# Decode step in one kernel: the last loads of K and V merged and put in the order K7, V6, V7

## The chip, the cores and the metric

The kernel runs on 1 core of one Trainium2 chip. The metric is device time in microseconds, the median of repeated runs. One further execution was recorded by the hardware profiler; all rows below come from it.

## The reference

One token of 512 elements passes through an attention block with a cache and a small feed-forward block, both under a modulation computed from `c`. Everything is bf16.

```python
mod = (_silu(c) @ w_mod).reshape(c.shape[0], 6, 1, -1)        # sa, ca, ga, sb, cb, gb
h = _layernorm(x) * (1 + ca) + sa
q = h @ wq                                                    # 32 query heads of 128
k, v = the caches of 8 heads, 32768 positions each, repeated 4 times
p = softmax(q k^T * 128 ** -0.5);  o = p v
x = x + ga * (o @ wo)                                         # wo: 4096 x 512
h = _layernorm(x) * (1 + cb) + sb
x = x + gb * (relu(h @ w1) @ w2)                              # w1: 512 x 1792, w2: 1792 x 512
```

K and V of one cache head are 8 MB each, so the 8 heads are 128 MB; w_mod, wq, wo, w1 and w2 together are some 15 MB.

## The kernel before, in words

**The stream of loads.** All large loads are issued by SyncE (SP) from one list, `stream` (L162 to L169), one after the other, through `load` (L112) and `stream_dma` (L154; the issue itself is L155). They go into a ring of three buffers of 8 MB (`piece`, L106): w_mod and wq share the first, then come K and V of the heads, and the last buffer, `tail_sb`, takes wo, w1 and w2. A load is issued when the buffer's former content has been used up. Which buffer that is follows from the order: K7 follows V4, V6 follows K6, V7 follows V5, and `tail_sb` follows K7. A head's K or V has four quarters (`u` = 0 to 3). Heads 0 to 4 are loaded whole, K5 too; K6, V5, K7 and V6 are loaded in halves, V7 in a half and two quarters. K7 and V6 alternate: K7's first half, V6's first half, K7's second, V6's second. wo comes in four transfers (4, 2, 1 and 1 heads, `WOP`, L47), w1 in one, w2 in five (`W2P`, L52).

**K0's second half** is loaded in three pieces (`UNEVEN`, L57 and L137 to L142): all but the last 512 bytes of each row, then these bytes of 111 rows, then those of the other 17. The vectors c and x come in one transfer each, issued by ScalarE (ACT, L183).

**One head.** VectorE (DVE) turns K in place (`turn_k`, L441), a quarter at a time, of K7 an eighth at a time. TensorE (PE) forms the scores with 16 matmuls for a quarter (`scores`, L460). `softmax` (L468) takes the maximum (L473; for K7 a maximum of each bank, L466, and then L475), sends it over the partitions (L478, L492), takes the exponential on ACT (L497), turns the result on DVE (L502) and sums it (L506, L509). Then PE multiplies with V, 16 matmuls for a quarter (`pv`, L523). `blocks` (L552, L556) scales the outcome on DVE, `o_cols` (L560) puts it in columns, and once all heads of a part of wo are done, `normalise` (L574) and `spread` (L586, L590) prepare it for that part.

**The order of work.** PE and DVE follow the order of the program from L637 on, written out by hand. In the loop over heads 0 to 5, head g+1's scores come before head g's `pv`. Then head 7 and 6 follow by hand (L675 to L708): K7's first two quarters are turned and scored, PE does `pv` of V6's first two quarters (L691), K7's other quarters follow, then head 7's softmax with the rest of V6 around it, and then V7.

**The end.** `project(i)` multiplies part i of wo: the first two parts into rows (L599), the other two into columns (L605), and `join_rows` (L614; L617, L622) turns the rows and adds them to the columns. Behind that come the residual (L740, L741, tile x1T), the second layer norm, w1 (L765), the relu (L775, L776), w2 (L788) and the output (L793, L795, L796). `keep_clock(n)` (L630, L635) puts n spare matmuls between these steps, whose results are not used.

Of the kernel before, what the change touches and what calls it, by code (L numbers as in the profile page):

```python
# [17 lines left out]
def kernel(  # L18
# [14 lines left out]
    nc = tc.nc  # L33
    P = 128
    _, _, D = A_x.shape
    _, Hkv, Sk, Dh = A_k_cache.shape
# [6 lines left out]
    TK = 64  # L43
    NTILE = Sk // (P * TK)
    NG = NTILE // 2

    WOP = [(0, Hkv // 2), (Hkv // 2, Hkv // 4), (Hkv - 2, 1), (Hkv - 1, 1)]  # L47
    WOROWS = 2
    LAST = Hkv - 1
    LOOPED = Hkv - 2  # L50
    HALVED = LOOPED - 1
    W2P = [(0, 5), (5, 10), (10, 12), (12, 13), (13, 14)]  # L52
    W1P = [(0, KT)]

    OUT0, OUT1 = 30, 34

    UNEVEN, EDGE, MOST = ("k", 0, (2, 3)), 2 * TK * Dh - D // 2, 111  # L57
    SPACE = 14
    assert Dh == 128 and REP == 4 and D == 512 and FT == W2P[-1][1] and NTILE == 4
    scale = float(Dh) ** -0.5  # L60
# [101 lines left out]
    whole, halves = [(0, 1, 2, 3)], [(0, 1), (2, 3)]  # L162
    stream = [("k", 0, halves[0]), ("wm",), ("wq",), ("k", 0, halves[1])]
    for g in range(LOOPED):
        stream += [("k", g + 1, s) for s in (halves if g >= HALVED else whole)] + [("v", g, s) for s in (halves if g >= HALVED else whole)]
    for s in halves:
        stream += [("k", LAST, s), ("v", LOOPED, s)]
    stream += [("v", LAST, (0, 1)), ("v", LAST, (2,)), ("v", LAST, (3,))] + [("wo", i) for i in range(len(WOP))]
    stream += [("w1", i) for i in range(len(W1P))] + [("w2", i) for i in range(len(W2P))]  # L169
    pos = [0]  # L170

# [8 lines left out]
    wm_sb = need(("wm",))  # L180
    cx_row = const.tile([16, D // 8], BF16)
    for i, row in enumerate((c[0], A_x[0, 0])):
        nc.scalar.dma_start(out=cx_row[8 * i:8 * i + 8], in_=row.rearrange("(a n) -> a n", a=8))  # L183

    ident_bf = const.tile([P, P], BF16)
    make_identity(nc, ident_bf[:])
# [10 lines left out]
        out=sel.rearrange("p (h par) (a c) -> p h par a c", h=2, a=4),  # L197
        in_=AP(ib.tensor, ib.offset, [ib.ap[0], [64, 2], [1, 2], [0, 4], [2, 32]]),
# [8 lines left out]
        out=mask16.rearrange("p (s q) -> p s q", q=REP),  # L207
        in_=AP(ident_f[:].tensor, ident_f[:].offset, [ident_f[:].ap[0], [0, 4], [1, REP], [REP, P // REP]]),
# [4 lines left out]
    for n in sorted({n * REP for _, n in WOP}):  # L213
        cmask[n] = const.tile([P, P // n], F32, name=f"cmask{n}")
        nc.vector.tensor_reduce(
            out=cmask[n][:], in_=ident_f[:].rearrange("p (c r) -> p c r", r=n), op=ALU.add, axis=AX.X,
# [3 lines left out]
            out=rsel_f[:], in_=ident_f[:].rearrange("p (c r) -> p r c", r=n), op=ALU.add, axis=AX.X,  # L220
# [6 lines left out]
        out=smask[:], in_=ident_f[0:16, 0:16].rearrange("p (s q) -> p s q", q=REP), op=ALU.add, axis=AX.X,  # L227
# [7 lines left out]
        out=place32[:], in_=ident_f[:].rearrange("p (j m) -> p m j", m=32), op=ALU.add, axis=AX.X,  # L235
# [4 lines left out]
        out=rowpick[:, OUT0:OUT1], in_=ident_f[:].rearrange("p (j m) -> p j m", m=32), op=ALU.add, axis=AX.X,  # L240
# [8 lines left out]
        out=cx_bd, in0=cx_row[:].unsqueeze(1).to_broadcast([16, 8, D // 8]),  # L249
# [23 lines left out]
    def row_bank(t):  # L273

        nc.vector.memset(t, 0.0)
        return t
# [85 lines left out]
    def four_rows(e, name):  # L362
# [16 lines left out]
        out=nca[:], in0=modT_sb[:, KT:2 * KT], scalar1=-1.0, scalar2=-1.0, op0=ALU.mult, op1=ALU.add,  # L379
# [3 lines left out]
        out=ncb[:], in0=modT_sb[:, 4 * KT:5 * KT], scalar1=-1.0, scalar2=-1.0, op0=ALU.mult, op1=ALU.add,  # L383
# [18 lines left out]
    for i in range(2):  # L402
        nc.vector.transpose(out=q_cols[:, i, :], in_=q_ps[i])
        nc.scalar.copy(
            out=qT_sb[:, 16 * i:16 * (i + 1)], in_=q_cols[:, i, :].rearrange("p (h r) -> p h r", r=32)[:, :, 0],
# [109 lines left out]
    def pv(g, us, js=range(16)):  # L515

        nb = 4 if g == HALVED - 1 else 1

        PT_g = PT_tiles[g][:].rearrange("p (h j c) -> p h (j c)", h=2, c=32)
        Vs = [need(("v", g, u)) for u in us]  # L520

        def step(u, V, PT, Vx, first=False):
            nc.tensor.matmul(o_tiles[g][:], lhsT=PT, rhs=Vx, start=first, stop=False, skip_group_check=True)  # L523

        Vf = [V.rearrange("p (s j) d -> p s (j d)", s=4) for V in Vs]
        if looped(g, us):

            with tc.tile_critical() as section:
                last_loop[:] = loop[:] = [section.name]
                with nc.tensor.Fori(0, 512 - 32 * nb + 1, 32 * nb) as at:  # L530
                    for b in range(nb):
                        for u, V in zip(us, Vf):
                            step(u, V, PT_g[:, u // 2, 32 * b + 16 * (u % 2):][:, bass.DynSlice(at, 16)],
                                 V[:, :, Dh * b:][:, :, bass.DynSlice(at * (Dh // 32), Dh)])
        else:
            for u, V in zip(us, Vf):
                for j in js:
                    c0 = 32 * j + 16 * (u % 2)
                    step(u, V, PT_g[:, u // 2, c0:c0 + 16], V[:, :, Dh * j:Dh * (j + 1)], (u, j) == (0, 0))
# [8 lines left out]
    def blocks(g):  # L548

        o = o_tiles.pop(g)[:].rearrange("p (s d) -> p s d", s=4)  # L550
        Y = spool.tile([16, Dh], F32, tag="Y", name="Y", bufs=1)
        nc.vector.scalar_tensor_tensor(  # L552
            out=o, in0=o, scalar=Linv_tiles.pop(g)[:], in1=smask[:].unsqueeze(2).to_broadcast([16, 4, Dh]),
            op0=ALU.mult, op1=ALU.mult,
        )
        nc.vector.tensor_reduce(out=Y[:], in_=o.rearrange("p s d -> p d s"), op=ALU.add, axis=AX.X)  # L556
        Y_tiles[g] = Y
# [24 lines left out]
    def spread(i):  # L582

        n = WOP[i][1] * REP
        o2_ps = small_ps([P, n], "o2_ps")
        nc.tensor.matmul(  # L586
            o2_ps[:], lhsT=oA[i][:].rearrange("p h c -> p (h c)"), rhs=rsel[n][:], start=True, stop=True,
        )
        o2 = const.tile([P, n], BF16, name=f"o2_sb{i}")
        nc.vector.tensor_copy(out=o2[:], in_=o2_ps[:])  # L590
        o2_tiles[i] = o2

    def project(i):

        n = WOP[i][1] * REP
        wo_sb = need(("wo", i))
        for r in range(n):
            if i < WOROWS:
                nc.tensor.matmul(  # L599
                    a_rows[0][32 * (r % 4):32 * (r % 4) + 1, :], lhsT=o2_tiles[i][:, r:r + 1],  # L600
                    rhs=wo_sb[:, r, :], start=False, stop=(i == WOROWS - 1 and r >= n - 4), skip_group_check=True,
                )
                continue
            for ko in range(KT):
                nc.tensor.matmul(  # L605
                    attnT_ps[:, ko:ko + 1],
                    lhsT=wo_sb[:, r, :].rearrange("p (m ko) -> p ko m", ko=KT)[:, ko, :],
                    rhs=o2_tiles[i][:, r:r + 1], start=False, stop=(i == len(WOP) - 1 and r == n - 1),
                    skip_group_check=True,
                )  # L610
# [3 lines left out]
    def join_rows():  # L614

        aT = room("tail_sb", TAIL, [P, 512])
        nc.vector.transpose(  # L617
            out=aT.rearrange("p (a ko m) -> p a ko m", a=4, ko=KT),
            in_=a_rows[0].rearrange("p (a m ko) -> p a ko m", a=4, ko=KT),
        )  # L620
        for a in range(4):
            nc.tensor.matmul(  # L622
                attnT_ps[32 * a:32 * a + 32, :], lhsT=place32[:],
                rhs=aT.rearrange("p (a ko m) -> p a ko m", a=4, ko=KT)[:, a, :, 0],
                start=False, stop=False, skip_group_check=True,
            )
# [3 lines left out]
    def keep_clock(n):  # L630

        if not spare:
            spare.append(bank("spare_ps"))
        for _ in range(n):
            nc.tensor.matmul(spare[0], lhsT=ident_bf[:], rhs=qbd[0][:, :, 0:P], start=True, stop=True)  # L635

    with tc.manual_schedule(engines={mybir.EngineType.PE, mybir.EngineType.DVE}):  # L637
# [37 lines left out]
        g, h = LOOPED, LAST  # L675
# [12 lines left out]
        normalise(g - 1)  # L688
        spread(part_of(g - 1))
        bank_max(h, 0)  # L690
        pv(g, (0, 1))  # L691
        for u in (2, 3):
            for half in range(2):
                turn_k(h, u, half)
# [3 lines left out]
        next(soft)  # L698
        next(soft)
        next(soft)  # L700
        pv(g, (2,), range(6))
        next(soft)
        next(soft)
        open_o(LAST)
        pv(g, (2,), range(6, 16))
        pv(g, (3,))
        next(soft)
        next(soft, None)  # L708
        end_b.append(two_banks("end_ps"))
        a_rows.append(row_bank(end_b[0][:, 0, :]))  # L710
        blocks(g)
        pv(LAST, (0, 1))
        o_cols(LAST - 1)
        normalise(LAST - 1)
        pv(LAST, (2,))
        spread(2)
        hid_ps = ps_o.tile([P, 512], F32, tag="o", name="hid_ps")
        nc.vector.memset(hid_ps[:], 0.0)
        pv(LAST, (3,))
# [6 lines left out]
        keep_clock(2)  # L726
        project(1)
        normalise(LAST)
        spread(3)
        keep_clock(2)  # L730
        project(2)
        keep_clock(1)
        join_rows()
        keep_clock(1)
        project(3)


        stat2 = const.tile([P, 2], F32)
# [3 lines left out]
            out=x1T[:], in0=x1T[:], scalar=1.0, in1=xT, op0=ALU.mult, op1=ALU.add, accum_out=stat2[:, 0:1],  # L742
# [31 lines left out]
        for f0, f1 in ((0, FT // 2), (FT // 2, FT)):  # L774
            nc.vector.transpose(out=hidT[:, f0:f1], in_=hid_v[:, f0:f1])  # L775
            nc.scalar.activation(  # L776
                out=AP(hb.tensor, hb.offset + 32 * f0 + 31, [hb.ap[0], [32, f1 - f0]]),
                in_=hidT[:, f0:f1, 0], func=ACT.Relu,
            )

        for part, (f0, f1) in enumerate(W2P):
            w2_sb = need(("w2", part))
            for ft in range(f0, f1):
                for i in (0, 2, 1, 3):
                    row = OUT0 + i
# [41 lines left out]
```

## Time and profile before

| | us |
|---|---|
| median of 3 runs | 354.11 (354.06 to 354.18) |
| the profiled execution, its own time | 354.42 |
| its span, first to last instruction | 352.6 |
| PE busy / DVE busy / ACT busy | 272.3 / 195.6 / 18.7 |
| mean rate of the loads | 424 GB/s, 149.42 MB read |

The span starts at 0 in all rows. Rows of the timeline give start, duration, engine, line, operation, output and inputs and, in brackets, how long the engine was idle before and what released it. "x32" is the count of merged instructions; the duration of such a row runs from the first to the end of the last.

### The profile page before, as it was taken

To read this page: it belongs to the slowest core of one execution; us is meant where nothing else is said; L and a number is where in the kernel's file an instruction comes from. 1 tells how busy PE (TensorE), PEld (TensorE's weight loads), DVE (VectorE), ACT (ScalarE), POOL (GpSimd) and SP (SyncE) were. 2 spreads that over 40 slices of the span, in tenths; PEclk is the share of its full clock that TensorE was granted. 3 is DMA by queue.
4 is the path that set the end of the run, shared out by engine and by line. 5 is a ranking of instruction groups with operands and counts; after the bars stand their busy time and mean duration, and the time that the engine had idled before them with its cause. 6 is when DMAs were issued, how large, how long until landed. Compare 5 with 4: busy or idle time off the path is not lost. (4 is left out here: it accounts for less than half of the span.)

```text
span 352.6 us, 3544 instructions
## 1 busy us (share of the span) xinstructions
PE 272.3 (77%) x1310; PEld 111.8 (32%) x1310; DVE 195.6 (55%) x167; ACT 18.7 (5%) x37; POOL 6.0 (2%) x26
## 2 busy tenths in 40 slices
PE   0054980695999679884988499976999999789994
PEld 0021330232333224331333233322444443234442
DVE  7662563983079513965099316956674293743142
ACT  1200003001000010001000100001000100011000
POOL 3000000000000000000000000000000000000000
PEclk9996895698999969998999979996999999999999
DMA  8999989999999999999999999999999999999995
GB/s 353 404 432 456 468 387 461 446 401 446 439 424 440 416 439 446 401 455 446 409 453 446 409 453 431 426 394 439 446 414 427 450 429 424 431 453 398 432 426 213
DMA packets 5222, 149.57 MB, mean 424 GB/s; under 512 B 604, under 2 KB 988, under 8 KB 1628
## 3 DMA queue, kind: packets, MB, share of 16 engines
q1 hardware_dynamic: 5180, 149.43, 98.5%
q8 instruction: 8, 0.13, 0.1%
q14 instruction: 2, 0.02, 0.0%
q10 hardware_dynamic: 32, 0.00, 0.0%
HBM read 149.42 MB, written 0.00 MB: 424 GB/s over the span
## 5 line engine op out<-in xcount | busy, mean ns | idle before, releaser
L441 DVE STREAM_TRANSPOSE Ksb<-Ksb 128x4096 f32<-128x4096 f32 (+1 forms) x34 | 131.5, 3912 | 57.6 <-DMA Ksb<-in_A_k_cache_dram 57.6
L460 PE MATMUL S_ps<-Ksb,qbd 128*128 128x512 bf16 x512 | 118.9, 385 | 19.2 <-DVE Ksb L441 18.3
L523 PE MATMUL o_ps<-Vsb,P_g 128*16 (+1 forms) x512 | 124.3, 401 | 10.9 <-ACT P_g L497 10.0
L460 PEld LDWEIGHTS <-qbd 128*128 128x128 bf16 x512 | 49.2, 97 | 84.9 <-issue 27.6
L523 PEld LDWEIGHTS o_ps<-Vsb,P_g 128*16 x320 | 30.4, 95 | 60.0 <-issue 31.8
L523 PEld LDWEIGHTS <-P_g 128*16 128x16 bf16 x192 | 16.7, 90 | 22.9 <-issue 0.4
L473 DVE TENSOR_REDUCE m_p<-S_ps 128x1 f32<-128x1024 f32 x7 | 8.6, 1223 | 21.8 <-PE S_ps L460 21.8
L502 DVE STREAM_TRANSPOSE P_g<-P_g 128x1024 bf16<-128x1024 bf16 x8 | 10.0, 1245 | 15.6 <-ACT P_g L497 15.6
L494 ACT ACTIVATE nbias<-Mb_ps 128x1 f32<-128x1 f32 x8 | 1.4, 171 | 269.5 <-PE Mb_ps L492 269.5
L324 PE MATMUL mod_ps<-wmq_sb,siluT 128*1 128x512 bf16 x24 | 3.6, 624 | 9.9 <-DMA wmq_sb<-in_w_mod_dram 9.9
L332 DVE STREAM_TRANSPOSE Ksb<-Ksb 128x4096 f32<-128x4096 f32 x2 | 8.8, 4424 | 1.7 <-DMA Ksb<-in_A_k_cache_dram 1.7
L478 PE MATMUL mT_ps<-ident_f,m_p 128*1 128x128 f32 x8 | 2.2, 270 | 8.9 <-DVE m_p L473 7.9
L497 ACT ACTIVATE P_g<-S_ps,nbias 128x1024 bf16<-128x1024 f32 x8 | 8.9, 1114 | 0.2
L560 PE MATMUL acc_ps<-mask_sb,Y 16*128 16x4 f32 x16 | 3.4, 282 | 5.1 <-DVE Y L556 5.1
L552 DVE SCALAR_TENSOR_TENSOR o_ps<-o_ps,Linv,smask 16x512 f32<-16x512 f32 x8 | 5.8, 720 | 2.8 <-PE o_ps L523 2.8
L254 PE MATMUL xc_ps<-cx_sel,wmq_sb 16*128 16x2 bf16 x4 | 0.3, 172 | 8.7 <-DVE wmq_sb L248 8.7
L590 DVE CAST o_sb<-o_ps 128x4 bf16<-128x4 f32 (+2 forms) x4 | 0.7, 167 | 11.1 <-PE o_ps L586 11.1
L415 POOL TENSOR_TENSOR qbd<-qrep_sb,rowpick 128x64 bf16<-128x64 bf16 x8 | 2.4, 299 | 228.0 <-PE S_ps L460 198.3
L509 DVE RECIPROCAL Linv<-L_ps 16x1 f32<-16x1 f32 x8 | 1.0, 126 | 8.3 <-PE L_ps L506 8.3
L556 DVE TENSOR_REDUCE Y<-o_ps 16x128 f32<-16x512 f32 x8 | 5.4, 679 | 0.3
L635 PE MATMUL spare_ps<-qbd,ident_bf 128*128 128x512 bf16 x18 | 5.4, 381 | 0.0
L396 PE MATMUL q_ps<-wmq_sb,hT 128*1 128x512 bf16 x32 | 3.6, 626 | 2.3 <-DMA wmq_sb<-in_A_wq_dram 2.3
(114 smaller groups left out, 71.6 us busy)
## 6 DMA issues: line engine op xcount, KB each, us to landing
Ksb<-in_A_k_cache_dram SPq DMA_DIRECT2D x5, 4096.0 KB, 22.9
Vsb<-in_A_v_cache_dram SPq DMA_DIRECT2D x5, 4096.0 KB, 36.5
wmq_sb<-in_A_wq_dram SPq DMA_DIRECT2D x1, 4096.0 KB, 28.1
Vsb<-in_A_v_cache_dram SPq DMA_DIRECT2D x2, 2048.0 KB, 41.1
Ksb<-in_A_k_cache_dram SPq DMA_DIRECT2D x1, 4032.0 KB, 37.2
wmq_sb<-in_w_mod_dram SPq DMA_DIRECT2D x1, 3072.0 KB, 18.9
tail_sb<-in_A_wo_dram SPq DMA_DIRECT2D x1, 2048.0 KB, 23.2
tail_sb<-in_B_w_dram SPq DMA_DIRECT2D x1, 1792.0 KB, 30.6
```

What stands on the lines that cost most here:

```text
L324: nc.tensor.matmul(dst[j // 4][32 * (j % 4):32 * (j % 4) + 1, :], lhsT=src_T[:, kt:kt + 1], rhs=w[:, kt, j * 512:(j + 1) * 512], start=(kt ...
L332: nc.vector.transpose(out=t, in_=t)
L396: nc.tensor.matmul(q_ps[i][32 * a:32 * a + 1, :].rearrange("o (h e) -> o h e", e=32), lhsT=hT[:, kt:kt + 1], rhs=wq_f[:, kt, i, a], start= ...
L441: t = nc.vector.transpose(out=KTt.bitcast(F32), in_=KTt.bitcast(F32))
L460: nc.tensor.matmul(S_ps_tiles[g], lhsT=qbd[g % 2][:, hp, 4 * (7 - s):4 * (7 - s) + P], rhs=KTv[:, 16 * sl:16 * sl + 16, h, :, par], start= ...
L473: behind_loop(nc.vector.reduce_max(out=m_p[:], in_=S_g.rearrange("p g f -> p (g f)"), axis=AX.X))
L497: nc.scalar.activation(out=P_g[:], in_=S_g.rearrange("p g f -> p (g f)"), func=ACT.Exp, bias=nbias[:], scale=scale, accum_out=l_g[:],)
L502: behind_loop(nc.vector.transpose(out=P_g[:], in_=P_g[:]))
L523: nc.tensor.matmul(o_tiles[g][:], lhsT=PT, rhs=Vx, start=first, stop=False, skip_group_check=True)
L552: nc.vector.scalar_tensor_tensor(out=o, in0=o, scalar=Linv_tiles.pop(g)[:], in1=smask[:].unsqueeze(2).to_broadcast([16, 4, Dh]), op0=ALU.m ...
L556: nc.vector.tensor_reduce(out=Y[:], in_=o.rearrange("p s d -> p d s"), op=ALU.add, axis=AX.X)
L635: nc.tensor.matmul(spare[0], lhsT=ident_bf[:], rhs=qbd[0][:, :, 0:P], start=True, stop=True)
```

## The change

Loads: K of head 6 and V of head 5 become one transfer each. The end of the list is K7, V6, V7 in halves, without alternating, and V7's second half is one transfer. wo comes in three transfers (4, 2 and 2 heads), w2 in four. K0's last bytes are split into 123 and 5 rows. c comes in three transfers and x in four. The number of transfers in all stays 40.

Compute: `pv` of V6's first half is taken out of its place between K7's quarters; the two quarters are multiplied around head 7's softmax, where the second two were, and those come behind it. The third part of wo now holds two heads: one `spread` less, one `project` less, and the part's 32 column matmuls stand behind `join_rows` and six spare matmuls.

```diff
-    WOP = [(0, Hkv // 2), (Hkv // 2, Hkv // 4), (Hkv - 2, 1), (Hkv - 1, 1)]
+    WOP = [(0, Hkv // 2), (Hkv // 2, Hkv // 4), (Hkv - 2, 2)]
...
-    W2P = [(0, 5), (5, 10), (10, 12), (12, 13), (13, 14)]
+    W2P = [(0, 6), (6, 11), (11, 13), (13, 14)]
...
-    UNEVEN, EDGE, MOST = ("k", 0, (2, 3)), 2 * TK * Dh - D // 2, 111
+    UNEVEN, EDGE, MOST = ("k", 0, (2, 3)), 2 * TK * Dh - D // 2, 123
...
     for g in range(LOOPED):
-        stream += [("k", g + 1, s) for s in (halves if g >= HALVED else whole)] + [("v", g, s) for s in (halves if g >= HALVED else whole)]
-    for s in halves:
-        stream += [("k", LAST, s), ("v", LOOPED, s)]
-    stream += [("v", LAST, (0, 1)), ("v", LAST, (2,)), ("v", LAST, (3,))] + [("wo", i) for i in range(len(WOP))]
+        stream += [("k", g + 1, whole[0]), ("v", g, whole[0])]
+    stream += [(x, g, s) for x, g in (("k", LAST), ("v", LOOPED), ("v", LAST)) for s in halves]
+    stream += [("wo", i) for i in range(len(WOP))]
...
-        nc.scalar.dma_start(out=cx_row[8 * i:8 * i + 8], in_=row.rearrange("(a n) -> a n", a=8))
+        for a, n in ((0, 2), (2, 2), (4, 2), (6, 2)) if i else ((0, 3), (3, 3), (6, 2)):
+            nc.scalar.dma_start(
+                out=cx_row[8 * i + a:8 * i + a + n], in_=row.rearrange("(a n) -> a n", a=8)[a:a + n],
+            )
...
         bank_max(h, 0)
-        pv(g, (0, 1))
         for u in (2, 3):
...
-        pv(g, (2,), range(6))
+        pv(g, (0,), range(6))
...
-        pv(g, (2,), range(6, 16))
-        pv(g, (3,))
+        pv(g, (0,), range(6, 16))
+        pv(g, (1,))
...
         a_rows.append(row_bank(end_b[0][:, 0, :]))
+        pv(g, (2, 3))
         blocks(g)
...
         pv(LAST, (2,))
-        spread(2)
...
         normalise(LAST)
-        spread(3)
-        keep_clock(2)
+        spread(2)
+        join_rows()
+        keep_clock(6)
         project(2)
-        keep_clock(1)
-        join_rows()
-        keep_clock(1)
-        project(3)
```

## The prediction

> **What bounds the kernel now.** I read the table of DMA queues first, then the chain of waits, then the timeline of the last 10 us, because the question is which engine sets the end.
>
> ```profile
> q1 hardware_dynamic: 5180, 149.43, 98.5%
> ```
> ```profile
> 338.50 11.12 DMA tail_sb<-in_B_w_dram
> ...
> 349.66 0.29 PE end_ps L788 x4
> ```
> ```profile
> 345.33 0.93 PE L765 MATMUL hid_ps<-tail_sb,h2T 128*1 128x448 bf16 x16 [1.28 <-DMA tail_sb<-in_B_w_dram]
> ...
> 347.10 0.61 PEld L788 LDWEIGHTS <-tail_sb 128*32 128x32 bf16 x21 [0.58 <-ACT tail_sb L776]
> ...
> 348.30 1.64 PE L788 MATMUL end_ps<-tail_sb 128*32 128x128 bf16 x36 [0.47 <-DMA tail_sb<-in_B_w_dram]
> ...
> 349.98 0.28 DVE L793 TENSOR_TENSOR o_rows<-end_ps,gb_rows 34x128 f32<-34x128 f32 x1 [2.95 <-PE end_ps L788]
> ```
>
> The stream of loads occupies its 16 engines for 98.5% of the span. The last piece of w2 lands at 338.50 + 11.12 = 349.62 and the last four matmuls start at 349.66. So the end is the end of the stream. But the margin is thin: TensorE (PE) was held by w1 for 1.28 us and by w2 for 0.47 us. If the work ahead of L765 and L788 becomes later than these slacks allow, PE sets the end. With w1 and w2 both there, L788 could have run earlier by about 1.3 + 0.5 = 1.8 us; PE delays up to about that are free, and what goes beyond is paid in full.
>
> ```profile
> 88.00:132.00 44.00, 36.93 (x152) 14.33 (x151) 22.18 (x12) 1.38 (x3) 0.30 (x1) 0.92 1.00 432
> ...
> 272.00:290.00 18.00, 17.69 (x85) 7.58 (x85) 11.61 (x12) 1.38 (x3) 0.00 (x0) 1.00 1.01 436
> ```
>
> These rows of the table by stretches (us, then busy us of PE, weight loads, DVE, ACT, POOL; clock, DMA share, GB/s) compare whole loads of 8 MB (88 to 132) with halves (272 to 290): 432 and 436 GB/s at a full DMA share. The size of these transfers doesn't set the rate, so merging them frees no time in the stream. PE is busy 17.69 of 18 us in the second: near the end of the kernel PE is nearly as full as the stream.
>
> **The change, part by part.**
>
> **K6 whole.** Now its first half lands early and VectorE (DVE) turns it while PE is still in the loop of the head before.
>
> ```profile
> 176.31 8.77 DVE L441 STREAM_TRANSPOSE Ksb<-Ksb 128x4096 f32<-128x4096 f32 x2 [10.78 <-DMA Ksb<-in_A_k_cache_dram]
> ```
> ```profile
> 214.85 8.77 DVE L441 STREAM_TRANSPOSE Ksb<-Ksb 128x4096 f32<-128x4096 f32 x2 [10.74 <-DMA Ksb<-in_A_k_cache_dram]
> ...
> 236.05 1.23 DVE L473 TENSOR_REDUCE m_p<-S_ps 128x1 f32<-128x1024 f32 x1 [3.73 <-PE S_ps L460]
> ```
> ```profile
> 243.99 8.77 DVE L441 STREAM_TRANSPOSE Ksb<-Ksb 128x4096 f32<-128x4096 f32 x2 [1.86 <-DMA Ksb<-in_A_k_cache_dram]
> ...
> 257.91 14.08 PE L460 MATMUL S_ps<-Ksb,qbd 128*128 128x512 bf16 x64
> ...
> 272.16 1.22 DVE L473 TENSOR_REDUCE m_p<-S_ps 128x1 f32<-128x1024 f32 x1
> ```
>
> K4 (176.31) and K5 (214.85) were whole and DVE waited for each; they came 38.54 us apart, which is the time of two 8 MB loads. K6 whole therefore lands at about 214.85 + 38.54 = 253.39. From the start of K5's turning to the maximum over its scores were 236.05 - 214.85 = 21.20 us, since DVE turns a quarter in 4.4 us and PE's last quarter follows. So K6's maximum comes at 253.39 + 21.20 = 274.59 instead of 272.16: **+2.4 us**. PE, which had all 64 score matmuls back to back (14.08 us), will wait for DVE between quarters. V5 whole costs nothing: its first half is wanted only after K6's scores, at about 274.6, and two 4 MB loads behind K6 (38.54 / 4 = 9.6 us each) it has landed at 272.7. All that follows on both engines, through V5 and the first half of K7, moves by 2.4 us.
>
> **Order K7, V6, V7.** Here are the lines that carry most of the sum.
>
> ```profile
> 295.26 7.07 PE L523 MATMUL o_ps<-Vsb,P_g 128*16 128x512 bf16 x32
> ...
> 295.45 0.68 DVE L466 TENSOR_REDUCE m<-S_ps 128x1 f32<-128x512 f32 x1
> 301.96 8.89 DVE L441 STREAM_TRANSPOSE Ksb<-Ksb 128x2048 f32<-128x2048 f32 x4 [5.83 <-DMA Ksb<-in_A_k_cache_dram]
> ```
>
> DVE is done with the first bank at 295.45 + 0.68 = 296.13 and waits 5.83 us for K7's second half. With the new order this half is one 4 MB load earlier, at about 301.96 - 9.6 = 292.3, before DVE wants it. The wait goes, and what is late next is DVE itself: 296.13 + 2.43 = 298.56 instead of 301.96, **-3.4 us** for K7's scores, its softmax and all that hangs on it.
>
> But the first row is the price. While DVE waited, PE worked: 32 matmuls of V6's first two quarters, 7.07 us from 295.26, with V6's first half already there. In the new order V6's first half lands where K7's second did, at about 302, and these 32 matmuls are taken out of this place; PE idles while DVE turns (8.89 us, in which PE has 32 score matmuls). They return behind K7's softmax, where PE was full:
>
> ```profile
> 321.13 0.19 PE L506 MATMUL L_ps<-l_g,mask_sb 128*16 128x1 f32 x2
> ...
> 321.39 7.07 PE L523 MATMUL o_ps<-Vsb,P_g 128*16 128x512 bf16 x32
> ...
> 332.25 0.18 PE L586 MATMUL o_ps<-rsel,oA 128*128 128x4 bf16 x1
> ...
> 332.36 3.62 PE L523 MATMUL o_ps<-Vsb,P_g 128*16 128x512 bf16 x16
> ```
>
> L506 moves to 321.13 - 3.4 = 317.7. Behind it stood V7's 64 matmuls, packed; now 32 of V6 stand ahead of them: **+7.07 us**, less 0.11 (332.25 to 332.36) for the removed spread. V6 and V7 as the stream brings them are early enough: V7's last half ends where its last quarter did, before 332.36, and is now wanted at about 332.3 and 335.9. So the last of V7's matmuls end 7.07 - 3.40 - 0.11 = 3.56 us later: 335.98 + 3.56 = 339.54.
>
> **wo in 3 and the new end of PE's list.**
>
> ```profile
> 338.52 0.60 PE L599 MATMUL end_ps<-tail_sb,o_sb 128*1 128x512 bf16 x8
> ...
> 339.06 0.18 PE L586 MATMUL o_ps<-rsel,oA 128*128 128x4 bf16 x1
> ...
> 339.10 0.59 PE L635 MATMUL spare_ps<-qbd,ident_bf 128*128 128x512 bf16 x2
> 339.27 0.16 DVE L590 CAST o_sb<-o_ps 128x4 bf16<-128x4 f32 x1 [0.98 <-PE o_ps L586]
> 339.35 0.71 DVE L617 STREAM_TRANSPOSE tail_sb<-end_ps 128x512 f32<-128x512 f32 x1
> 339.74 0.61 PEld L605 LDWEIGHTS <-tail_sb 128*128 128x128 bf16 x16 [0.54 <-DMA tail_sb<-in_A_wo_dram]
> ...
> 341.71 0.16 DVE L740 TENSOR_TENSOR x1T<-acc_ps,modT_sb 128x4 f32<-128x4 f32 x1 [1.65 <-PE acc_ps L605]
> ```
>
> The spread of the last part stood at 339.06, and x1T started 2.65 us behind it, with 16 of the L605 matmuls on either side of the joining of rows. In the new list all 32 stand behind the joining and behind six spare matmuls (0.22 each, as the scores run). I add it up from the spread at 339.06 + 3.56 = 342.62, less about 0.15 because no row of wo is waited for any more ahead of L599: 342.5. Cast by +0.37 (339.06 to 339.27 + 0.16); joining transpose 0.71 to 343.6; its matmuls 0.24; six spares 6 x 0.22 = 1.3, to 345.15; 32 matmuls at about 0.035 (16 loads in 0.61, pipelined) 1.1 and 0.17 until the sum can be read. x1T starts at **346.4**, 4.7 us later than 341.71. The transfers of wo have all landed by then.
>
> **From x1T to the end.** L765 could have started at 345.33 - 1.28 = 344.05, 2.34 us behind x1T: now 346.4 + 2.34 = 348.75, with w1 there since 345.3. L788 followed L765 by 347.10 - 345.33 = 1.77: 350.5. Its 56 matmuls run at 0.029 each (21 weight loads in 0.61) as w2 is complete at 349.6: the last four start 52 x 0.029 = 1.5 later, at 352.0, and o_rows 0.32 behind them (349.66 to 349.98): 352.35 against 349.98, **+2.4 us**. What is behind o_rows stays.
>
> **w2 in 4, K0's split, c and x in 7.**
>
> ```profile
> SPq L155 <- DMA Vsb<-in_A_v_cache_dram: 15.5, 3, 6.3
> ...
> SPq L155 <- DMA tail_sb<-in_A_wo_dram: 6.6, 2, 4.5
> ```
>
> Three issues of w2 waited for V7's three pieces and two for wo's first two: each issue waits for the landing eight transfers before it. After the change the total is again 40 transfers, and the four of w2 wait for V6's and V7's halves, the last at about 331: earlier, and with a full queue ahead of them in both kernels. Worth 0, while the stream has work queued. In front, the same rule makes K0's later pieces and K1 wait for K0, w_mod or wq, the last at 29.8, while K0's second half is still to come; no gap.
>
> ```profile
> 7.99 0.68 DVE L248 TENSOR_TENSOR wmq_sb<-cx_row,pick 16x512 bf16<-16x512 bf16 x1 [1.50 <-DMA cx_row<-in_A_x_dram]
> ...
> 24.34 0.69 DVE L340 COPY wmq_sb<-mod_ps 128x512 f32<-128x512 f32 x1 [2.67 <-ACT wmq_sb L339]
> ...
> 29.79 3.58 PE L396 MATMUL q_ps<-wmq_sb,hT 128*1 128x512 bf16 x32 [2.31 <-DMA wmq_sb<-in_A_wq_dram]
> ```
>
> x may land about 6 us later, because its pieces wait for one another (x alone came at 7.99). Of this 2.67 + 2.31 us are hidden by these two waits, and the rest by DVE's 10.7 us of waiting for each later K; without that cover it would cost up to 1 to 6 us. The split of K0 by 123/5 moves 12 rows of 512 B among a few of the 16 engines, fractions of a microsecond on one engine. I take 0, with -0.5 to +0.5 as bounds for what this may do to the slowest engine's end, and it counts only if the stream sets the end.
>
> The sum, 2.4 us, stands against the profiled execution, 354.42 us (span 352.6): 356.8. That execution is 0.31 us above the median of 354.11, so I forecast **356.5 us**. Bounds of the terms: K6's landing is known to half a microsecond from the spacing of K4 and K5 (-0.5 to +0.5); of the new tail, the six spares may lie wholly within the wait for the joined rows (-1.3) or cost 0.3 each like the two in 0.59 (+0.5), and the 32 matmuls may run like two separate groups of 0.7 (+0.2). I take the values nearest to the rows and keep 355.0 to 357.7, a little wider on top as a late front adds.
>
> **Rivals.** (a) *The stream still ends last.* If PE's list were later by no more than the slack of about 1.8 us, w2's landing at 349.6 would set the end as before: 354.1, between 353.6 and 354.6. It decides at a lateness of L765 of 1.28 us (I have 4.7). For it: the stream is unchanged in bytes. Against it: 7.07 us of matmuls move from an idle place to a full one and only 3.4 us come back. (b) *The clock drops.* PE has a hole from about 298.1 (bank maximum at 295.45 + 2.43 = 297.9, which follows the scores and a spread) to 300.8 (298.56 and one eighth, 8.89 / 4 = 2.2), where before V6's matmuls stood.
>
> ```profile
> 197.40:202.80 5.40, 0.95 (x5) 0.50 (x4) 3.46 (x6) 1.38 (x3) 0.30 (x1) 0.85 0.98 425
> 204.60:208.00 3.40, 3.40 (x10) 1.08 (x9) 0.00 (x0) 0.00 (x0) 0.00 (x0) 0.50 0.89 386
> 302.00:304.30 2.30, 0.33 (x2) 0.10 (x1) 2.30 (x2) 0.00 (x0) 0.00 (x0) 1.00 1.05 456
> 340.00:345.00 5.00, 4.05 (x51) 1.99 (x48) 2.10 (x15) 0.29 (x1) 0.00 (x0) 1.00 0.99 422
> 345.00:348.00 3.00, 2.42 (x39) 1.14 (x40) 0.71 (x2) 0.47 (x2) 0.00 (x0) 1.00 1.00 400
> ```
>
> Behind a nearly idle stretch of 5.4 us the granted clock is 0.50; behind one of 2 us (302.0 to 304.3) it is 1.00. The new hole of 2.7 us is between them. At half clock eight score matmuls take some 3.4 us instead of 1.9, against DVE's 2.2: with one slow group of eight the scores end at 300.8 + 3.4 + 3 x 1.9 = 309.9, with two at 311.4, instead of 298.56 + 8.89 + 1.9 = 309.35: 0.5 to 2.0 us, 357.0 to 358.5. The Trainium skill ("TensorE: Matmul & The Clock Gate", Part 1) says that the clock halves after an idle window of about 3.4 us; by that rule the hole stays at full clock and the sum stands. (c) *Faster: fewer, larger transfers shorten the stream.* Had the 8 us from 340 to 348 run at 432 GB/s instead of 422 and 400, (5 x 10 + 3 x 32) / 432 = 0.3 us would be won, and 0.5 by evener engines: 353.3 to 353.9; only if (a) holds as well. The Trainium skill ("DMA: Bandwidth & Descriptors", Rules for kernel authors) advises to join small transfers into large ones, and its section Anatomy of one DMA puts the fixed part of one at about 2 us; by that, five transfers fewer on the stream might save up to 10 us, an estimate from that page; the two rows of 432 and 436 GB/s show no such part between queued loads.
>
> **How the numbers follow.** Forecast as summed: 0.62. (b): 0.18. (a): 0.10. (c): 0.05. A front that isn't hidden, above 358.5: 0.05. About 0.2% (0.7 us) is what a measurement can tell from no change. (a) is 0.07 within 0.2%, 0.02 below and 0.01 above; all of forecast, (b) and the late front is slower, (c) faster. Slower 0.86, same 0.07, faster 0.07. The range 354.9 to 358.5 leaves out (a), (c) and the late front.
>
> **What would show it.** Right: DVE's maximum over K6's scores about 2.4 us later; its wait for K7's second half gone; PE idle while K7's last quarters are turned; 32 matmuls of L523 behind L506 that weren't there; x1T near 346; L765 and L788 without waits for DMA, and w2 landing near 349.6 well before it is used. Wrong: L788 still released by a DMA, K6's maximum near 272, or a stream that ends elsewhere than 349.6.

## The result and the profile after

| | before | after |
|---|---|---|
| median of 6 runs, us | 354.14 | 356.63 |
| the profiled execution, its span | 354.42, 352.6 | 356.72, 354.8 |
| ratio, after to before | | 1.0069, 95% interval 1.0056 to 1.0083 |

The changed kernel is 2.5 us slower; 356.5 was forecast. One of its six executions took 365.92 us; such slow executions come up in several series below, of the kernel before too, and the ratios and ranges, though not the medians, leave them out.

Code of `turn_k` and what follows moved by two lines (L441 is L443, L523 is L525), that of the end by two the other way (L765 is L763, L788 is L786, L793 is L791).

From the table of DMA queues, and then the last pieces of the chain of waits (start, duration, what):

```profile
q1 hardware_dynamic: 4464, 149.43, 97.8%
```
```profile
343.86 1.40 PE spare_ps L637 x6
345.26 1.04 PE acc_ps L607 x32
...
348.67 0.92 PE hid_ps L763 x16
...
350.40 1.76 PE end_ps L786 x54
352.16 0.02 issue
352.18 0.29 DVE o_rows L791
```

The bytes are the same, the stream's share of the span is a little smaller, and the chain no longer ends in a transfer. Where before had `DMA tail_sb` up to 349.62, there are now PE's spare matmuls, wo's last part, w1 and w2 one behind the other. Two stretches of the timeline show how it came to that, DVE first and then PE:

```profile
253.90 8.77 DVE L443 STREAM_TRANSPOSE Ksb<-Ksb 128x4096 f32<-128x4096 f32 x2 [11.42 <-DMA Ksb<-in_A_k_cache_dram]
...
275.23 1.21 DVE L475 TENSOR_REDUCE m_p<-S_ps 128x1 f32<-128x1024 f32 x1
...
298.52 0.68 DVE L468 TENSOR_REDUCE m<-S_ps 128x1 f32<-128x512 f32 x1
299.12 8.88 DVE L443 STREAM_TRANSPOSE Ksb<-Ksb 128x2048 f32<-128x2048 f32 x4
...
339.66 0.75 DVE L554 SCALAR_TENSOR_TENSOR o_ps<-o_ps,Linv,smask 16x512 f32<-16x512 f32 x1 [12.10 <-PE o_ps L525]
...
346.33 0.16 DVE L738 TENSOR_TENSOR x1T<-acc_ps,modT_sb 128x4 f32<-128x4 f32 x1 [2.77 <-PE acc_ps L607]
...
352.18 0.28 DVE L791 TENSOR_TENSOR o_rows<-end_ps,gb_rows 34x128 f32<-34x128 f32 x1 [1.85 <-PE end_ps L786]
```
```profile
301.47 1.90 PE L462 MATMUL S_ps<-Ksb,qbd 128*128 128x512 bf16 x8 [3.08 <-DVE Ksb L443]
...
318.28 0.19 PE L508 MATMUL L_ps<-l_g,mask_sb 128*16 128x1 f32 x2
318.33 13.97 PE L525 MATMUL o_ps<-Vsb,P_g 128*16 128x512 bf16 x64
...
332.55 6.64 PE L525 MATMUL o_ps<-Vsb,P_g 128*16 128x512 bf16 x30
...
348.63 0.93 PE L763 MATMUL hid_ps<-tail_sb,h2T 128*1 128x448 bf16 x16
...
350.40 1.74 PE L786 MATMUL end_ps<-tail_sb 128*32 128x128 bf16 x56
```

K6's turning starts when the whole of K6 has landed. The turning of K7's second half (299.12) has no bracket: DVE goes on without waiting. PE, which had V6's matmuls there, is idle for 3.08 us. Behind L508 there are now 64 matmuls in one packed row where there were 32. L763 and L786 have no bracket either: neither waits for a load. The stream itself ends where it ended. Two stretches of the table (us, busy us of PE, weight loads, DVE, ACT, POOL; clock, DMA share, GB/s), of before and then of after:

```profile
349.00:349.25 0.25, 0.25 (x10) 0.20 (x8) 0.00 (x0) 0.00 (x0) 0.00 (x0) 1.00 0.20 66
349.25:350.00 0.75, 0.63 (x12) 0.25 (x7) 0.02 (x1) 0.00 (x0) 0.00 (x0) 1.00 0.00 0
```
```profile
349.00:349.25 0.25, 0.25 (x12) 0.09 (x4) 0.03 (x1) 0.00 (x0) 0.00 (x0) 1.00 0.19 66
349.25:350.00 0.75, 0.75 (x11) 0.21 (x3) 0.39 (x2) 0.00 (x0) 0.00 (x0) 1.00 0.00 0
```

In both kernels the last bytes of w2 move in the same quarter of a microsecond. Before had its last matmuls held by that transfer; after starts L786 at 350.40, some 0.8 us behind the 349.62 at which w2 had landed before.

### The profile page after: what moved, and what is told of

It reads as the page before. It is cut to its first block, busy times and chain, and to the rows that moved or that the text cites. A ratio compares the mean times of both kernels' runs of the same rounds, so it can differ in the third digit from the quotient of the medians.

```text
span 354.8 us, 3545 instructions
## 1 busy us (share of the span) xinstructions
PE 272.3 (77%) x1311; PEld 112.0 (32%) x1311; DVE 194.4 (55%) x163; ACT 18.7 (5%) x37; POOL 5.8 (2%) x25
## 5 line engine op out<-in xcount | busy, mean ns | idle before, releaser
L443 DVE STREAM_TRANSPOSE Ksb<-Ksb 128x4096 f32<-128x4096 f32 (+1 forms) x34 | 131.4, 3908 | 54.5 <-DMA Ksb<-in_A_k_cache_dram 43.6
L525 PE MATMUL o_ps<-Vsb,P_g 128*16 (+1 forms) x512 | 123.6, 401 | 10.8 <-ACT P_g L499 10.0
L525 PEld LDWEIGHTS o_ps<-Vsb,P_g 128*16 x320 | 30.4, 95 | 59.6 <-issue 30.7
L525 PEld LDWEIGHTS <-P_g 128*16 128x16 bf16 x192 | 16.8, 90 | 23.0 <-issue 0.2
L554 DVE SCALAR_TENSOR_TENSOR o_ps<-o_ps,Linv,smask 16x512 f32<-16x512 f32 x8 | 5.9, 734 | 18.3 <-PE o_ps L525 18.3
L347 PE MATMUL t_ps<-ident_f,wmq_sb 128*128 128x128 f32 x8 | 2.3, 438 | 6.0 <-DVE modT_sb L348 5.3
L483 DVE TENSOR_REDUCE Mrow<-mT_ps 1x4 f32<-1x128 f32 x8 | 2.2, 273 | 5.6 <-PE mT_ps L480 5.6
```

The costliest lines, as they stand in the source:

```text
L347: nc.tensor.transpose(out=t_ps[:, i, :], in_=rows[:, i, :], identity=ident_f[:])
L443: t = nc.vector.transpose(out=KTt.bitcast(F32), in_=KTt.bitcast(F32))
L554: nc.vector.scalar_tensor_tensor(out=o, in0=o, scalar=Linv_tiles.pop(g)[:], in1=smask[:].unsqueeze(2).to_broadcast([16, 4, Dh]), op0=ALU.m ...
```

## The experiments

Each is given as a change to one of the two kernels. "Halves" is the old line of the stream for K6 and V5; a hole is a stretch in which PE has no instruction.

**Order alone** (before, with the order K7, V6 and the moved `pv`):

```diff
-    for s in halves:
-        stream += [("k", LAST, s), ("v", LOOPED, s)]
+    stream += [(x, g, s) for x, g in (("k", LAST), ("v", LOOPED)) for s in halves]
...
-        pv(g, (0, 1))
```

> The kernel before with the new order alone (K7, V6, V7; the matmuls of V6's first half moved as in the change; K6 and V5 still in halves, wo, w2, K0, c and x as before). Theory (the two parts cost only together, by PE's slack): DVE starts K7's second half at 296.1 instead of 302.0, so K7's scores end 5.9 us earlier, 7.07 us of matmuls come back behind them: PE's list is 1.2 us late at the end of V7, which the wait of 1.28 us for w1 still covers; end set by w2's landing near 349.6, 354.1 to 354.4 us. Rival (the order is the whole cost): 356.0 to 356.6 us, L765 and L788 not waiting for a load.

354.29 us, ratio 1.0001 (0.9992 to 1.0010). The timeline of DVE and then of PE:

```profile
296.20 8.88 DVE L440 STREAM_TRANSPOSE Ksb<-Ksb 128x2048 f32<-128x2048 f32 x4
```
```profile
315.42 13.97 PE L522 MATMUL o_ps<-Vsb,P_g 128*16 128x512 bf16 x64
...
347.96 1.59 PE L787 MATMUL end_ps<-tail_sb 128*32 128x128 bf16 x36 [0.51 <-DMA tail_sb<-in_B_w_dram]
```

DVE starts 5.8 us earlier, PE gets the 64 packed matmuls, and the end still waits for w2. The order alone neither gains nor costs: what DVE wins is paid back by PE, and the rest stays within PE's slack.

**K6 and V5 whole alone** (before):

```diff
-        stream += [("k", g + 1, s) for s in (halves if g >= HALVED else whole)] + [...]
+        stream += [("k", g + 1, whole[0]), ("v", g, whole[0])]
```

> The kernel before with K6 and V5 whole and nothing else changed. Theory: K6's maximum 2.4 to 3 us later, V6's matmuls end near 304.7 instead of 302.3, and DVE's wait for K7's second half (landing at 302.0 as before) takes the delay up; K7's scores end within 0.5 us of 312.8, 354.1 to 354.4 us. Rival (K6 whole is the whole cost): 356.3 to 357.0 us, everything behind K6 2.4 us later.

354.71 us, ratio 1.0014 (1.0005 to 1.0024).

```profile
301.73 8.89 DVE L441 STREAM_TRANSPOSE Ksb<-Ksb 128x2048 f32<-128x2048 f32 x4 [3.05 <-DMA Ksb<-in_A_k_cache_dram]
...
349.60 0.28 DVE L793 TENSOR_TENSOR o_rows<-end_ps,gb_rows 34x128 f32<-34x128 f32 x1 [2.93 <-PE end_ps L788]
```

K6's lateness goes into DVE's wait for K7's second half, 3.05 us instead of 5.83, and o_rows is not later than before's 349.98. With the old order the merge costs no work on the path. The 0.5 us by which this kernel is slower, more than the theory allowed, appear behind o_rows (below, on the time after the output's issue).

**The changed kernel with K6 and V5 in halves.**

> The changed kernel with K6 and V5 in halves again. Theory: PE's whole list behind K6 is 2.9 us earlier than in the changed kernel, L763 at about 345.7, w2's landing (349.6) sets the end again: 354.1 to 354.5 us. Rival (the order, or the joined wo, costs by itself): 355.3 to 356.6 us.

355.71 us, ratio 1.0045 (1.0032 to 1.0058): a miss.

```profile
330.72 6.63 PE L525 MATMUL o_ps<-Vsb,P_g 128*16 128x512 bf16 x30 [1.29 <-DMA Vsb<-in_A_v_cache_dram]
...
348.57 1.74 PE L786 MATMUL end_ps<-tail_sb 128*32 128x128 bf16 x56
```

Of K6's 3.07 us only 350.40 - 348.57 = 1.83 come back. PE now reaches V7's second half too early, and this half is one transfer: it holds PE 1.29 us. In the changed kernel K6's lateness had covered that wait. Another 0.8 us lie behind o_rows.

**And V7's second half in quarters, c and x in two each** (40 transfers):

```diff
+    stream += [("v", LAST, (0, 1)), ("v", LAST, (2,)), ("v", LAST, (3,))]
```

> The changed kernel with K6 and V5 in halves and V7's second half in two quarters, and c and x in two transfers each, so that the number of transfers stays 40. Theory after the run with K6 and V5 in halves (there PE stood 1.29 us before V7's second half, and the last SP waits took 0.8 us longer): with both taken away L763 comes at about 345.5, w1 and w2 end the chain as in the kernel before, 354.0 to 354.5 us. Rival (joined wo and six spares cost by themselves): 355 us or more.

354.80 us, ratio 1.0022 (1.0010 to 1.0034), above the range of the theory and in two groups: eight executions at 354.41 to 354.94 and three at 356.07 to 356.45. The profiled one is of the second. Its timeline of PE, and the table by stretches (clock third from the right):

```profile
298.93 9.96 PE L463 MATMUL S_ps<-Ksb,qbd 128*128 128x512 bf16 x32 [3.08 <-DVE Ksb L444]
```
```profile
295.00:298.00 3.00, 0.85 (x5) 0.38 (x4) 2.11 (x3) 0.00 (x0) 0.00 (x0) 0.99 0.99 426
298.00:301.00 3.00, 2.07 (x5) 0.68 (x5) 3.00 (x3) 0.00 (x0) 0.00 (x0) 0.50 0.96 415
301.00:304.00 3.00, 3.00 (x8) 1.01 (x7) 3.00 (x3) 0.00 (x0) 0.00 (x0) 0.50 1.06 459
```

In the hole ahead of K7's scores the granted clock goes to 0.50, and PE falls behind DVE.

**The same, with the hole filled:**

```diff
         bank_max(h, 0)
+        keep_clock(10)
```

> The kernel with K6 and V5 in halves, V7 as a half and two quarters, c and x in two transfers each (40 transfers) and all six spare matmuls ahead of project(2), with ten more spare matmuls behind bank_max(h, 0), in PE's hole ahead of the scores of K7's second half. Without the ten it gave 354.41 to 354.94 in eight executions and 356.07 to 356.45 in three, and its profiled execution, one of the three, had the granted clock at 0.50 from 298 to 304 and the 32 score matmuls in 9.96 us. Theory (the second group is the clock lowered in this hole): the clock stays at 1.00 between 294 and 310, and all executions lie in 354.3 to 355.0. Rival (the clock goes down whatever PE does there, or the second group comes from another place): two to four of some ten executions at 356.0 to 356.5 again.

354.85 us, ratio 1.0017 (1.0008 to 1.0027), eleven executions from 354.62 to 355.16. PE, the stretches, and the end on PE and on DVE:

```profile
295.21 2.32 PE L638 MATMUL spare_ps<-qbd,ident_bf 128*128 128x512 bf16 x10
298.43 1.90 PE L463 MATMUL S_ps<-Ksb,qbd 128*128 128x512 bf16 x8 [0.90 <-DVE Ksb L444]
...
305.00 1.90 PE L463 MATMUL S_ps<-Ksb,qbd 128*128 128x512 bf16 x8 [0.29 <-DVE Ksb L444]
```
```profile
298.00:301.00 3.00, 2.28 (x10) 0.96 (x10) 3.00 (x3) 0.00 (x0) 0.00 (x0) 1.00 1.01 437
```
```profile
348.67 1.22 PE L788 MATMUL end_ps<-tail_sb 128*32 128x128 bf16 x32 [0.47 <-DMA tail_sb<-in_B_w_dram]
```
```profile
349.93 0.28 DVE L793 TENSOR_TENSOR o_rows<-end_ps,gb_rows 34x128 f32<-34x128 f32 x1 [2.64 <-PE end_ps L788]
```

The clock stays at 1.00, the scores take 305.00 + 1.90 - 298.43 = 8.47 us instead of 9.96, and the second group is gone (three of eleven against none of eleven, so chance alone is not excluded by the count; the clock in the profile is the stronger sign). And the end waits for w2 again: with K6 and V7 split, the rest of the change leaves the stream as the bound. The 0.6 us above the kernel before lie behind o_rows: the span ends 2.5 us after the issue of the output, in before 2.0.

**One spare matmul instead of six** (the changed kernel):

```diff
-        keep_clock(6)
+        keep_clock(1)
```

> The changed kernel with one spare matmul instead of six between the joining and the last part of wo. Theory: PE's list sets the end, so five matmuls of 0.22 us come off it: 1.1 us earlier, 355.3 to 355.7 us, L763 near 347.5. Rival (the stream or another engine sets the end): 356.4 to 356.9 us; if the clock drops without the spares, the matmuls behind them take twice as long and the gain is smaller.

Two executions at 355.21 and 355.41, as expected, and three at 356.52 to 356.99; median 356.57, ratio 1.0059 (1.0044 to 1.0075). The profiled one (355.21), on DVE:

```profile
339.23 0.75 DVE L554 SCALAR_TENSOR_TENSOR o_ps<-o_ps,Linv,smask 16x512 f32<-16x512 f32 x1 [12.09 <-PE o_ps L525]
...
344.82 0.16 DVE L738 TENSOR_TENSOR x1T<-acc_ps,modT_sb 128x4 f32<-128x4 f32 x1 [1.70 <-PE acc_ps L607]
```

x1T comes 1.51 us earlier; 0.43 of it was there before the spares (`blocks`, L554, at 339.23 instead of 339.66), 1.08 is the five spares. They stood on the path. The three later executions have no profile.

**The same, with the hole ahead of K7's scores filled** (`keep_clock(10)`, as above).

> The changed kernel with one spare matmul instead of six ahead of project(2), and ten spare matmuls behind bank_max(h, 0), in the 3.1 us in which PE has nothing before the scores of K7's second half. The same kernel without the ten gave 355.21 and 355.41 in two executions and 356.52 to 356.99 in three. Theory (the two groups are the granted clock: an execution that halves it in this idle stretch runs the 32 score matmuls in 10 us instead of 8.5): the hole is shorter than 1 us, the granted clock stays 1.00 between 297 and 310, and all executions lie within 355.1 to 355.7, median 355.3. Rival (the second group has another cause, or the clock is lowered whatever PE does there): executions remain at 356.4 to 357.0, and the median stays near 356. Second rival (ten matmuls are too many and delay K7's scores): all executions later by up to 0.5 us, 355.6 to 356.

355.29 and 355.44, and again 356.29 to 356.76 in three; median 356.41, ratio 1.0057 (1.0044 to 1.0070). The theory as put there fell: with only one spare at the end, a second group remains though the hole is filled. The profiled execution is of the first group, so this run does not show where the time goes in the others.

**K6 and V5 in halves, V7 in quarters, and one spare:**

> The changed kernel with K6 and V5 in halves, V7 as a half and two quarters, c and x in two transfers each (40 transfers), and one spare matmul instead of six ahead of project(2). With the six spares it gave 354.41 to 354.94, and 356.07 to 356.45 in three executions. Theory (with K6 early again the list of PE and the stream of weights end together; what is left is the stream's end at 349.6 and the work behind its last transfer): PE's list ends 1.1 us earlier, the lower executions don't go below 354.1, median 354.2 to 354.7, and the executions with the lowered clock come down by about 1 us, to 355.0 to 355.4. Rival (PE's list is still what ends last): 1.1 us less, 353.3 to 353.8, faster than the kernel before.

355.19 us (354.71 to 355.68), ratio 1.0028 (1.0017 to 1.0038), no faster than with six spares and above the range of the theory. PE, and the stretches:

```profile
345.75 1.48 PE L764 MATMUL hid_ps<-tail_sb,h2T 128*1 128x448 bf16 x16
```
```profile
344.00:346.00 2.00, 2.00 (x9) 0.43 (x12) 0.93 (x5) 0.29 (x1) 0.00 (x0) 0.50 0.97 396
```

With one spare the clock is at 0.50 from 344 to 346 here, and w1's matmuls take 1.48 us instead of 0.93. PE's longest idle stretch between 337 and 344 is 0.88 us, the wait for the joined rows; its instructions there are short ones. So this is a second place at which the clock can fall, though in the profiles of the two runs above, also with one spare, it stays at 1.00 there. That it is the second group's place in the two runs above is likely, but not shown.

**wo in four, the old end of PE's list, x in three** (the changed kernel otherwise):

```diff
-    WOP = [(0, Hkv // 2), (Hkv // 2, Hkv // 4), (Hkv - 2, 2)]
+    WOP = [(0, Hkv // 2), (Hkv // 2, Hkv // 4), (Hkv - 2, 1), (Hkv - 1, 1)]
```

> The changed kernel with wo in four transfers and PE's end of the list as before (two spreads, one spare on either side of the joining, 16 column matmuls ahead of it); x in three transfers, so that the count stays 40. Theory: from the last spread to x1T 2.65 instead of 3.8 us, so x1T at about 345.3 and the end 1.0 to 1.1 us earlier than the changed kernel: 355.4 to 355.8 us. Rival (wo's part of the list is hidden): 356.4 to 356.9 us.

355.56 to 356.04 in four executions and 357.16 and 357.26 in two; median 355.90, ratio 1.0050 (1.0033 to 1.0066). The profiled one (357.16) has the lowered clock, its 32 scores take 10.04 us. Its timeline of PE:

```profile
319.40 0.19 PE L508 MATMUL L_ps<-l_g,mask_sb 128*16 128x1 f32 x2
```

L508 is 1.12 us later than in the changed kernel, and yet x1T starts at 346.31, as there (346.33): the old end is 1.1 us shorter. So the new end of PE's list is 1.1 us of the loss. wo in three transfers and the new end of the list were not run apart.

**c and x in one transfer each** (the changed kernel, 35 transfers).

> The changed kernel with c and x in one transfer each, as before; the waits of w2's issues keep their places, since the count falls ahead of all of them. Theory (the late front is hidden): x is used near 8 us instead of 17.3, V0 is issued near 35.4 instead of 39.0, K2's start and all later loads don't move, and the end stays at 356.4 to 356.9 us. Rival (the late front is part of the loss): 353.0 to 355.5 us.

356.77 us, ratio 1.0077 (1.0064 to 1.0090), as the changed kernel; five executions at 356.50 to 356.78 and one at 358.06. First its first use of x on DVE, then that of the changed kernel:

```profile
8.09 0.68 DVE L247 TENSOR_TENSOR wmq_sb<-cx_row,pick 16x512 bf16<-16x512 bf16 x1 [2.07 <-DMA cx_row<-in_A_x_dram]
```
```profile
17.32 0.68 DVE L250 TENSOR_TENSOR wmq_sb<-cx_row,pick 16x512 bf16<-16x512 bf16 x1 [11.32 <-DMA cx_row<-in_A_x_dram]
```

The pieces make x 9.2 us later, and nothing of it reaches the end. Behind c and x this kernel is the changed kernel, and here the clock did fall in the hole ahead of K7's scores; its stretches, and PE:

```profile
301.00:304.00 3.00, 2.86 (x7) 0.97 (x7) 3.00 (x3) 0.00 (x0) 0.00 (x0) 0.50 1.11 481
304.00:307.00 3.00, 3.00 (x15) 1.33 (x14) 3.00 (x2) 0.00 (x0) 0.00 (x0) 0.97 0.88 382
```
```profile
301.14 8.58 PE L459 MATMUL S_ps<-Ksb,qbd 128*128 128x512 bf16 x32 [3.07 <-DVE Ksb L440]
```

It came back early enough to cost only 0.1 us (8.58 instead of 8.47).

**K0's split 123/5 alone** (before).

> The kernel before with the split of K0's uneven transfer alone changed, from 111 and 17 rows to 123 and 5. Theory (the front is covered by the stream of weights, and the end is set by its last transfer): no difference, 354.0 to 354.4, ratio 0.999 to 1.001. Rival (the uneven split brings K0 earlier or the queues start differently, and the stream ends earlier or later by the same time): a difference of 0.3 to 1 us either way.

354.20 us, ratio 0.9999 (0.9989 to 1.0008): no difference.

**c and x in two each** (before, 42 transfers).

> The kernel before with c and x in two transfers each: 42 transfers instead of 40, nothing else. Theory of the closing waits (SP waits for the last landing on each of eight semaphores in a fixed order; with 40 transfers the output's is the last of them, with 42 it comes ahead of five others): the span's end comes 0.5 to 0.9 us later behind the output's issue, 354.6 to 355.0 us. Rival (the number of transfers is indifferent, as the prediction had it): 354.0 to 354.3 us.

355.24 us, ratio 1.0027 (1.0017 to 1.0037), slower as the theory had it and by a little more. Its o_rows comes at 349.77, before's at 349.98; the time is behind it. SP's issue of the output and SP's waits at the end (us, times, longest), of this kernel and then of before:

```profile
350.40 0.29 SPq L800 DMA_DIRECT2D out_dram<-o_bf  x1
```
```profile
SPq L826 <- DMA out_dram<-o_bf: 0.9, 1, 0.9
```
```profile
350.61 0.29 SPq L796 DMA_DIRECT2D out_dram<-o_bf  x1
```
```profile
SPq L822 <- PEq L822: 0.6, 2, 0.4
```

From the output's issue to the end of the span are 353.2 - 350.4 = 2.8 us, before 352.6 - 350.6 = 2.0. SP's last waits contain one for the output that before doesn't show. That wait alone is not the cause: the changed kernel has one of 0.5 us, and ends 2.0 us after the issue as before does. So two more transfers of a few hundred bytes, hidden at the front, cost 0.8 us at the end; that their count does it is not shown.

## Why the prediction was right

The mechanism was right: PE's list, late by more than its slack, took the end over from the stream. The terms of the sum, one by one:

**K6 whole**: right in kind, somewhat too small in size. The maximum came 275.23 - 272.16 = 3.07 us later, not 2.4: K6 landed at 253.90 instead of 253.39, and the stretch behind it was 21.33 us instead of 21.20. Part of that is scatter between executions: in two other kernels with K6 whole it landed at 253.35 (K6 and V5 whole alone) and 253.56 (c and x in one transfer each). The -3.4 us of the order contain K6's delay (5.83 less 2.43); that with the old order the wait would have hidden all of it was not said. Nor was it in the working that a wait for V7 stands behind it: "early enough" was true of V7's merged half only because K6 is late.

**Order K7, V6, V7**: DVE's wait of 5.83 us went; L508 came at 318.28 (317.7 forecast), so the gain is 2.85 us, not 3.4, by K6's 0.6. Behind it the 64 matmuls were packed, and V7 ended 0.4 us sooner after L508 than summed: `blocks` started at 339.66 against 339.54 for the last matmuls. That the two errors nearly cancel is luck.

**wo in 3 and the new end**: x1T at 346.33 (346.4). The six spares, costed at 0.22 each, took 345.10 - 343.79 = 1.31 us from their start to that of the matmuls behind them; five of them are 1.08 by experiment.

**From x1T to the end**: L763 at 348.63 (348.75), L786 at 350.40 (350.5), o_rows at 352.18 (352.35). No wait for a DMA in any of them. PE's slack was larger than the 1.8 us of the prediction's first part: x1T was 346.33 - 341.71 = 4.62 us late and o_rows 2.20, so 2.4 us were free. The sentence with 1.8 leaves out that before's last 36 matmuls of L788 took 1.64 us, where 36 x 0.029 are 1.05; the sum itself had all 56 at full pace and came out right. In the same way the bound of rival (a), 1.28 us at L765, is too tight: with the hole filled L765 started 345.59 - 344.05 = 1.54 us late, and the end still waited for w2.

**w2 in 4, K0's split, c and x in 7**: 0, as forecast, in this sum (w2 in four was not run alone); x is 9.3 us later than before and not 6. The working took the count of 40 for harmless, and in this kernel it was: both end 2.0 us after the issue of the output. Other counts cost 0.3 to 0.8 us there (2.3 us with 35 transfers, 2.7 with 38, 2.8 with 42), which the working did not have. The count isn't the whole of it: with 40 transfers in other divisions it was 2.2 (wo in four) and 2.5 (350.56 to 353.1, the hole filled). What decides is left open.

**The rivals.** (a), the stream still ends last, is what happens once K6, V5 and V7 are split: of the loss, 2.25 us (o_rows 352.18 to 349.93, there with the hole filled) go with these merges, and without them the slack holds, the new end of PE's list (1.1 us by the run with wo in four) included. Without the filled hole the lower group, at 354.41 to 354.94, is no slower.

(b), the clock, did not happen in the changed kernel's profile, whose four groups of scores take 1.90 us each, and its executions at 356.33 to 357.00 show no second group. It fell in five of the eight profiled executions that have this hole of 3.07 to 3.08 us (2.7 forecast), so its absence in this one is luck; in the kernel with K6 and V7 split it cost 9.96 - 8.47 = 1.5 us, inside the 0.5 to 2.0 that were worked out. The rule of the Trainium skill ("TensorE: Matmul & The Clock Gate", Part 1) that the clock halves after an idle window of about 3.4 us would have kept it away; the clock fell in a hole of 3.08 us, some 2 us into it (0.99 over 295 to 298, PE's last matmul ending at about 295.9, then 0.50), in some executions and not in others. There the measurement decides.

(c), fewer transfers make the stream faster, has no support: with 32 transfers on the stream instead of 37 its last bytes move in the same quarter of a microsecond (the stretches at 349). The advice of "DMA: Bandwidth & Descriptors" of the Trainium skill (Rules for kernel authors) is to join small transfers; the pieces of wo and w2 that were joined have 128 KB and more, and no run here shows a saving. The 2 us that the prediction takes from that page's section Anatomy of one DMA are given there for transfers issued by GpSimd; these are issued by SP.

No version ran faster than the kernel before. The nearest, K0's split and the order alone, are equal to it (354.20 and 354.29): where the stream ends last, no run shows a part of this change that shortens it.

## What to carry to other kernels

Where a stream of loads sets the end by a margin of some 2 us, sum what every edit adds to the other engine's list, in its order, and compare with that margin: here the order alone and the merge of K6 and V5 alone leave o_rows where it was, and the whole change moves it by 2.2 us. A wait that an edit hides comes back when the edit is undone, so undo in pairs before a term is believed. And before spare matmuls that look like waste are taken out, read the granted clock in that place.

## What the runs showed of the hardware

- The granted clock halved around an idle stretch of PE of 3.07 to 3.08 us in five of eight profiled executions, and stayed at 1.00 in the other three (the order alone, the changed kernel, the changed kernel with one spare). It fell 2.1 to 3.8 us after PE's last matmul, in two cases when PE was already busy again. It stayed at 0.50 for some 3.3 us in three of them, which cost 0.1 to 0.3 us of the 32 scores, and for some 6.8 us in two (K6 and V7 split; wo in four), which cost 1.5 and 1.6. Both of these two executions belong to the slower group of their kernel. Ten spare matmuls in the stretch kept it at 1.00 in the two profiles with them. Of the three short ones, the kernel with K6 and V5 in halves, its stretch and its timeline (8.79 instead of 8.47 for the scores):

```profile
298.00:301.00 3.00, 3.00 (x9) 1.12 (x9) 3.00 (x2) 0.00 (x0) 0.00 (x0) 0.61 1.01 437
```
```profile
297.97 8.79 PE L462 MATMUL S_ps<-Ksb,qbd 128*128 128x512 bf16 x32 [3.08 <-DVE Ksb L443]
```

- The time from the issue of the output to the end of the span is not constant: 2.0 to 2.8 us in these kernels, with another number or division of the transfers. Two more small transfers at the front moved it by 0.8 us.
